# Full attention's value products in pieces of 256 queries, and a choice between streams that counts ScalarE's reserve

## The chip, the cores and the metric

The kernel runs on one core of one Trainium2 chip. The metric is the device time of one execution in microseconds, the median of several runs. TensorE (PE in the profile) multiplies, ScalarE (ACT) takes the exponentials, VectorE (DVE) and GpSimd (POOL) do the rest of the arithmetic, SyncE (SP) issues most of the transfers.

## The reference

Four layers stand one behind the other on a sequence of 2048 rows of 512 numbers. Each takes a layer norm of its input and adds its result to it. Layers one and three (A) are full attention with 32 heads of 16 numbers, where all heads share one key and one value head. Layers two and four (B) have 32 heads with keys and values of their own. They go through the sequence in four segments of 512: causal attention within the segment, mixed by a gate for each head with a linear-attention memory of the segments before.

```python
def _A_ref(x, wq, wk, wv, wo):
    q = (x @ wq).reshape(B, S, H, Dh).transpose(0, 2, 1, 3)
    k = x @ wk
    v = x @ wv
    p = softmax(einsum("bhqd,bkd->bhqk", q, k) * Dh ** -0.5)
    o = einsum("bhqk,bkd->bhqd", p, v)
    return o.transpose(0, 2, 1, 3).reshape(B, S, H * Dh) @ wo

# B, for each of 4 segments s of L = 512
p = softmax(einsum("bhqd,bhkd->bhqk", qs, ks) * scale + mask)
a_dot = einsum("bhqk,bhkd->bhqd", p, vs)
a_mem = (phi(qs) @ M) / (phi(qs) @ z + 1e-6)
outs.append(g * a_mem + (1.0 - g) * a_dot)
M = M + einsum("bhld,bhle->bhde", phi(ks), vs)
z = z + einsum("bhld->bhd", phi(ks))

x = x + _A_ref(layernorm(x), ...)
x = x + _B_ref(layernorm(x), ...)
x = x + _A_ref(layernorm(x), ...)
x = x + _B_ref(layernorm(x), ...)
```

## The kernel before

**Two streams.** The program is written by Python generators that emit instructions, and two streams of them are woven together. The first is full attention, on blocks of 512 queries. It is itself two generators. `a_scores` takes a block, four heads and a tile of 128 keys at a time; for each pair of heads it emits eight matmuls (a score group, `qa,kst` in the profile, written by `by_pairs` at L99 and L102) into a pair of PSUM banks, and one exponential of 128x1024 on ScalarE (L751) into a buffer `pa`. `a_products` then multiplies the exponentials of one key tile with the values: eight fp32 matmuls of 64 keys x 17 columns by 512 queries (`pa,va`, in `a_pv` from L772), which add up over 16 key tiles in two PSUM banks of their own. There are 2048 score groups and 1024 products. The second stream, `side`, does all else for one block of 512 rows: the output projection and layer norm (`out_norm`), layer B's segment (`b_block`: projections, the row maxima `b_rowmax` that VectorE reduces at L988, and `b_attend` with its own scores, masks, exponentials at L1027 and value products `pa,vb`), layer B's output projection, and the next full-attention layer's projections (`a_prep`). A projection is twelve matmuls of 128x128 by 512 (`xh,w`, `xl,w` or `w,xh`, `w,xl`, L454).

**Stages.** Stage 0 weaves block 0 of full attention with the preparation of all blocks. In stages 1 to 7 full attention works on one block while `side` works on the block before. The last `side` runs by itself. Within a stage two pairs of PSUM banks hold scores (`layout("ab")`), and nine buffers hold exponentials. A rule in `a_scores` (`gate`, L721) lets full attention begin only the first unit of the next stage's block before that stage has begun.

**What sets the order.** Every generator yields before a piece of work, with a function that says when the piece could begin by clocks that the Python code keeps for each engine (`clk`). A `Need` carries besides the form of TensorE's array that the piece uses: "rows" (64 rows by 32 columns, for scores and value products of full attention), "cols" (128 rows by 32 columns, for the value products of layer B) or "full". `step` (L410) takes the generator whose piece can begin first, with 260 ns added where the form changes, and a term for the lag of one stream behind the other. `par` (L386) does the like within the second stream. So the order of instructions is fixed when the program is built; on the chip each engine works through its own queue in that order and waits on semaphores. In that order one product is one piece of 8 matmuls, and a projection two pieces of 6 (a yield at `kt == 1`).

Of the kernel before, what the change touches and what calls it, by code (L numbers as in the profile page):

```python
# [89 lines left out]
def net_kernel(ctx, tc, x_in, a_wq, a_wk, a_wv, a_wo, b_wq, b_wk, b_wv, b_wo, b_beta, cst, out):  # L90
# [75 lines left out]
    DRAIN = 130.0  # L166
    PVL = 0.0
    PEND = 0.0
    clk = {"pe": 0.0, "act": 0.0, "dve": 0.0, "pool": 0.0}
# [187 lines left out]
    rings = {}  # L357
# [13 lines left out]
    class Need:  # L371


        def __init__(self, at, form):
            self.at, self.form_ = at, form

# [3 lines left out]
        def form(self):  # L380
            return self.form_() if callable(self.form_) else self.form_

    def form_of(need):
        return need.form() if isinstance(need, Need) else "full"

    def par(*gens):  # L386


        live = []
        for g in gens:  # L390
            if g is not None:
                try:
                    live.append([g, next(g)])
                except StopIteration:
                    pass

        def pick():
            ready = [z for z in live if z[1]() <= clk["pe"]]
            same = [z for z in ready if form_of(z[1]) == tiling[0]]
            return (same or ready or [min(live, key=lambda z: z[1]())])[0]  # L400

        while live:
            yield Need(lambda: min(z[1]() for z in live), lambda: form_of(pick()[1]))
            z = pick()
            try:
                z[1] = next(z[0])
            except StopIteration:
                live = [y for y in live if y is not z]

    def step(zs, cost):  # L410

        now = clk["pe"]
        best = None
        for z in zs:
            if z[1] is None:
                continue
            at = z[1]()
            s = max(now, at) + (2 * DRAIN if form_of(z[1]) != tiling[0] else 0.0) + cost(z)
            if best is None or s < best[0]:
                best = s, at, z  # L420
# [24 lines left out]
    def project(out_, lhs_h, lhs_l, rhs_h, rhs_l, need):  # L445

        yield lambda: max(need(), rings["r"].ready())
        i, ps = rings["r"].take()
# [3 lines left out]
        for kt in range(4):  # L452
# [3 lines left out]
            end = pe(660)  # L456
            if kt == 1:
                yield lambda: 0.0
        def release(t):
# [257 lines left out]
    def a_scores(units):  # L717
# [11 lines left out]
        for ui, (L, f, b, n, k0, k1) in enumerate(units):  # L729
# [8 lines left out]
            for kt in range(k0, k1):  # L738
                pe_, te = [], []
                for u in range(2):  # L740
                    yield Need(lambda: max(need, rings["sc"].ready(), exps.ready(), L["kr"][kt // 4], gate(f, n, k1)), form)
                    ring = rings["sc"]
# [21 lines left out]
    def a_products(n):  # L764

        for _ in range(n):
            yield Need(lambda: max(queue[0][-1], pva_free[0] if queue[0][1] else 0.0) if queue else 1e18, "rows")
            a_pv(*queue.pop(0))

    a_ob = {}  # L770

    def a_pv(L, first, kt, x, unit, last, _):  # L772
        f_, b, n, k0, k1 = unit
        gone[f_] = gone.get(f_, 0) + 1
        t, p = divmod(n, 2)
        for j in (2, 3, 0, 1):
            for h in range(2):
                w_ = slice(64 * h, 64 * h + 64)
                together(j == 2 and h == 0, pva[32 * j:32 * j + 17, h, :], lhsT=L["va"][w_, kt, 0:17],
                         rhs=x[j // 2][0][w_, j % 2, :], start=first, stop=last)  # L780
        e = pe(860, "rows")
        for _, i in x:
# [216 lines left out]
    def b_attend(b, n, r, last):  # L999
# [4 lines left out]
        for kt in range(4):  # L1004
            nq = 512 - kt * P
            es, loc = [], ([(0, 0), (1, 0)] if kt < 2 else [(0, 0), (0, nq)])
            for s_ in range(1 if kt >= 2 else 2):
                yield Need(lambda: max(gr[n], rings["sc"].ready(), exps.ready()), "cols" if exact else "rows")
                ring = rings["sc"]
# [22 lines left out]
        pvb, rel = yield from slot(None, max(tl, v_r[0]), "cols")  # L1032
        for part in parts:
            b_pv(t, p, pvb, *part)
        for i in held:
# [242 lines left out]
```

## Time and profile before

| | us |
|---|---|
| median of 3 runs (3176.38 to 3182.36) | 3179.75 |
| the profiled execution's own time | 3173.99 |
| its span, first to last instruction | 3172.1 |
| TensorE busy, whole span | 2799.0 |
| ScalarE busy, whole span | 2325.2 |
| stage 0 and the preparation (0 to 336.8) | 336.8 |
| stages 1 to 7 (336.8 to 2981.3), each | 362.6 to 397.0 |
| the last block's second stream alone (2981.3 on) | 190.8 |

The granted TensorE clock is 0.975 of full speed on average; in the stages it is 0.97 to 1.00, in the last stretch 0.84. Stage boundaries are taken where each 256th exponential of full attention ends.

How to read it: the trace names an engine, a line, what is written and read, and the count. An fp32 matmul of the program stands in the trace as two, one behind the other, so a value product shows as two passes of eight matmuls. The length of a matmul's row holds the way through the array too, so that the distance from one group's start to the next is its price, not its length. L99 marks the first matmul of a group, L102 the rest.

### The profile page before, as it was taken

What the parts mean: (1) busy time and instruction counts of PE and PEld (TensorE: products, weight loads), DVE (VectorE), ACT (ScalarE), POOL (GpSimd) and SP (SyncE); (2) the same over time, 40 slices, a digit from 0 to 9 for tenths busy, and PEclk for the clock granted to TensorE, in tenths of its full rate; (3) what the DMA queues carried; (4) which work ended last, traced back from release to release, by engine and by line L of the source; (5) the groups of instructions that cost most, each with busy time, mean ns of one, the idle gap of its engine ahead of it and who ended that gap; (6) DMA issues with size and microseconds to landing.
All of it is one profiled execution on the core that took longest, in us unless ns stands there. A gap on an engine that the chain in (4) does not pass through costs nothing.

```text
span 3172.1 us, 116270 instructions
## 1 busy us (share of the span) xinstructions
PE 2799.0 (88%) x51714; PEld 1329.8 (42%) x51714; DVE 1656.8 (52%) x4599; ACT 2325.2 (73%) x2583; POOL 396.0 (12%) x569
## 2 busy tenths in 40 slices
PE   6988898899888998889998898988998889988987
PEld 4533344345333454434443343443443334433544
DVE  7621355545655456556465454565445535555465
ACT  4699787876778767787778768668687876878523
POOL 2100010012100121002110020210110003100011
PEclk9999999999999999999999999999999999999978
DMA  4310121012210132102221132311221104311331
GB/s 124 99 42 22 46 63 43 25 50 78 67 39 18 54 91 58 35 15 73 89 63 46 33 108 66 92 47 34 84 63 31 48 12 160 95 48 33 114 106 34
DMA packets 138560, 194.11 MB, mean 61 GB/s; under 512 B 29664, under 2 KB 97088, under 8 KB 138048
## 3 DMA queue, kind: packets, MB, share of 16 engines
q1 hardware_dynamic: 118912, 121.56, 13.1%
q0 software_dynamic: 19136, 65.02, 7.2%
q8 instruction: 407, 6.67, 0.9%
q14 instruction: 105, 0.86, 0.1%
HBM read 126.46 MB, written 60.03 MB: 59 GB/s over the span
## 4 chain that ended last, share of the span: by engine, by line
PE 38%; ACT 31%; issue 15%; DVE 10%; DMA 3%; POOL 2%; SPq 0%; DVEq 0%; ACTq 0%; POOLq 0%
ACT pa L751 28%; PE bank L99 16%; PE bank L454 13%; PE bank L102 7%; DVE mo L988 4%; ACT pa L1027 3%; DVE m L959 1%; POOL w L186 1%; POOL parts L550 1%; DMA xt<-in_A_x_dram 1%; DMA wst<-in_B_wk_dram 1%; PE bank L514 1%; DMA wst<-in_B_wq_dram 1%; DVE parts L552 0%; DVE qf L532 0%
## 5 line engine op out<-in xcount | busy, mean ns | idle before, releaser
L751 ACT ACTIVATE pa<-bank 128x1024 f32<-128x1024 f32 x2048 | 1945.1, 1113 | 470.0 <-PE bank L102 465.5
L102 PE MATMUL bank<-pa,va 64*17 64x512 f32 x14336 | 1107.4, 601 | 0.2 <-DVE t L790 0.2
L99 PE MATMUL bank<-pa,va 64*17 64x512 f32 x2048 | 1065.5, 601 | 15.8 <-DVE ts L789 9.2
L99 PE MATMUL bank<-qa,kst 49*32 49x512 f16 x2048 | 746.1, 383 | 179.4 <-ACT pa L751 150.3
L102 PE MATMUL bank<-qa,kst 49*32 49x512 f16 x14336 | 827.9, 388 | 0.6 <-DVE xt L835 0.6
L988 DVE CUSTOM_DVE_ANT_0 mo<-bank,maskq 128x256 bf16<-128x256 f32 (+3 forms) x896 | 437.9, 489 | 209.5 <-PE bank L102 145.0
L102 PEld LDWEIGHTS <-kst 49*32 49x32 f16 x14336 | 227.5, 90 | 509.5 <-issue 498.7
L99 PE MATMUL bank<-qkb 48*32 48x128 f16 (+7 forms) x1536 | 346.4, 311 | 104.4 <-DVE m L988 46.0
L1027 ACT ACTIVATE pa<-bank 128x1024 f32<-128x1024 f32 (+2 forms) x384 | 323.7, 887 | 127.5 <-PE bank L102 125.1
L102 PE MATMUL bank<-qkb 48*32 48x384 f16 (+7 forms) x6656 | 369.9, 313 | 0.0
L99 PEld LDWEIGHTS <-kst 49*32 49x32 f16 x2048 | 174.3, 92 | 364.9 <-issue 340.3
L454 PE MATMUL bank<-xh,w 128*128 128x512 f32 x832 | 286.7, 409 | 11.6 <-DVE w L318 4.8
L102 PEld LDWEIGHTS bank<-pa,va 64*17 64x17 f32 x14336 | 259.4, 95 | 24.7 <-DVE t L790 8.8
L186 POOL TENSOR_SCALAR w<-wst 128x512 fp32r<-128x512 f32 x160 | 108.4, 679 | 1189.5 <-PE bank L454 1033.3
L454 PE MATMUL bank<-w,xh 128*128 128x512 f32 x752 | 246.7, 408 | 2.5 <-DVE xh L825 1.1
L102 PEld LDWEIGHTS <-qkb 48*32 48x32 f16 (+1 forms) x6656 | 152.8, 94 | 211.6 <-issue 202.6
L99 PEld LDWEIGHTS bank<-pa,va 64*17 64x17 f32 x2048 | 186.7, 94 | 105.7 <-DVE ts L789 14.5
L789 DVE STREAM_TRANSPOSE ts<-bank 128x512 f32<-128x512 f32 x88 | 62.8, 714 | 279.1 <-PE bank L102 278.9
L99 PEld LDWEIGHTS <-qkb 48*32 48x32 f16 (+1 forms) x1536 | 130.1, 96 | 155.0 <-issue 124.5
L454 PEld LDWEIGHTS bank<-xh,w 128*128 128x128 f32 x832 | 158.7, 191 | 80.0 <-issue 30.9
L1038 DVE STREAM_TRANSPOSE t<-bank 128x512 f32<-128x512 f32 x64 | 45.8, 715 | 273.6 <-PE bank L102 273.6
L102 PE MATMUL bank<-pa,vb 128*17 128x384 f32 (+3 forms) x1920 | 171.4, 442 | 8.5 <-ACT pa L1027 7.6
(164 smaller groups left out, 2987.5 us busy)
## 6 DMA issues: line engine op xcount, KB each, us to landing
sb<-parts SPq DMA_DIRECT2D x128, 128.0 KB
qkb<-sb SPq DMA_DIRECT2D x256, 64.0 KB
x<-xt SPq DMA_DIRECT2D x48, 256.0 KB
xt<-x SPq DMA_DIRECT2D x48, 256.0 KB
qa<-sd SPq DMA_DIRECT2D x176, 66.0 KB
wd<-w POOLq DMA_DIRECT2D x20, 512.0 KB, 3.7
w<-wd POOLq DMA_DIRECT2D x18, 512.0 KB, 6.1
xt<-in_A_x_dram SPq DMA_DIRECT2D x32, 256.0 KB
```

The costliest lines, as they stand in the source:

```text
L99: nc.tensor.matmul(*a, **k)
L102: tc.keep_in_program_order(nc.tensor.matmul(*a, **k))
L186: G.tensor_scalar(o, i, 1.0, 0.0, op0=ALU.mult, op1=ALU.add)
L454: T.matmul(ps, lhsT=l_(kt), rhs=r_(kt), start=n == 0, stop=n == 11)
L514: T.transpose(ps[:, k, :], xn[:, k * P:(k + 1) * P], ident)
L550: G.tensor_scalar(parts[:, 0, :], x, up, 0.0, op0=ALU.mult, op1=ALU.add)
L751: A.activation(x, sc, AF.Exp, scale=scale)
L789: V.transpose(ts.rearrange("p a b -> p (a b)"), pva[:, 0, :])
L959: V.reduce_max(m[:, u0:u0 + per, i, qt], ps[:, 0:per * nk].rearrange("p (h k) -> p h k", k=nk), axis=AX.X)
L988: V.tensor_tensor_reduce(out=mo[:, 0:nk], in0=ps[:, o_:o_ + nk], in1=maskq[:, 512 - nk:512], op0=ALU.add, op1=ALU.max, scale=1.0, scalar=- ...
L1027: A.activation(e[:, :, 0:w], sc[:, :, 0:w], AF.Exp, scale=0.25 if exact else 0.25 / (UPB * UPB))
L1038: V.transpose(t1.rearrange("p a b -> p (a b)"), pvb)
```

## The change

**Products in halves.** `a_products` emits a product in two pieces of 256 queries with a yield between them, except for the first product of a unit, which clears the PSUM region and stays whole. The new `a_part` writes a piece; `a_pv` keeps what comes after.

**A cost and a mark for each piece.** A `Need` now also says how long its piece keeps TensorE (`cost_`; 1320 ns where nothing is said) and whether it feeds ScalarE (`feeds_`: scores of both attentions).

**The choice.** `step` works out when ScalarE would be dry, `dry`: 400 ns (`AHEAD`) before ScalarE's clock, or, where later, the time at which a feeding piece can begin. A piece that doesn't feed ScalarE gets 0.3 (`STARVE`) of the time by which its end would pass `dry` added to its score.

**Other yields.** A projection still yields after the second of its four key tiles (`PIECE = 2`). `b_attend`'s value products yield before key tiles 1 and 2 (`BRK`).

```diff
@@ -165,6 +165,10 @@
     LAG = 0.03
     DRAIN = 130.0
     PVL = 0.0
+    PIECE = 2
+    BRK = (1, 2)
+    STARVE = 0.3
+    AHEAD = 400.0
     PEND = 0.0
     clk = {"pe": 0.0, "act": 0.0, "dve": 0.0, "pool": 0.0}
     evac_on = ["dve"]
@@ -371,14 +375,22 @@
     class Need:
 
 
-        def __init__(self, at, form):
-            self.at, self.form_ = at, form
+        def __init__(self, at, form, cost=400.0, feeds=False):
+            self.at, self.form_, self.cost_, self.feeds_ = at, form, cost, feeds
 
         def __call__(self):
             return self.at()
 
         def form(self):
             return self.form_() if callable(self.form_) else self.form_
+
+    def cost_of(need):
+        c = need.cost_ if isinstance(need, Need) else 1320.0
+        return c() if callable(c) else c
+
+    def feeds(need):
+        c = need.feeds_ if isinstance(need, Need) else False
+        return c() if callable(c) else c
 
     def form_of(need):
         return need.form() if isinstance(need, Need) else "full"
@@ -400,7 +412,8 @@
             return (same or ready or [min(live, key=lambda z: z[1]())])[0]
 
         while live:
-            yield Need(lambda: min(z[1]() for z in live), lambda: form_of(pick()[1]))
+            yield Need(lambda: min(z[1]() for z in live), lambda: form_of(pick()[1]), lambda: cost_of(pick()[1]),
+                       lambda: feeds(pick()[1]))
             z = pick()
             try:
                 z[1] = next(z[0])
@@ -411,11 +424,17 @@
 
         now = clk["pe"]
         best = None
+        dry = 1e18
+        for z in zs:
+            if z[1] is not None and feeds(z[1]):
+                dry = min(dry, max(z[1](), clk["act"] - AHEAD))
         for z in zs:
             if z[1] is None:
                 continue
             at = z[1]()
             s = max(now, at) + (2 * DRAIN if form_of(z[1]) != tiling[0] else 0.0) + cost(z)
+            if not feeds(z[1]):
+                s += STARVE * max(0.0, max(now, at) + cost_of(z[1]) - dry)
             if best is None or s < best[0]:
                 best = s, at, z
         s, at, z = best
@@ -444,7 +463,7 @@
 
     def project(out_, lhs_h, lhs_l, rhs_h, rhs_l, need):
 
-        yield lambda: max(need(), rings["r"].ready())
+        yield Need(lambda: max(need(), rings["r"].ready()), "full", 330.0 * PIECE)
         i, ps = rings["r"].take()
         ring = rings["r"]
         ps = out_(ps)
@@ -454,8 +473,8 @@
                 T.matmul(ps, lhsT=l_(kt), rhs=r_(kt), start=n == 0, stop=n == 11)
                 n += 1
             end = pe(660)
-            if kt == 1:
-                yield lambda: 0.0
+            if kt < 3 and kt % PIECE == PIECE - 1:
+                yield Need(lambda: 0.0, "full", 660.0 * PIECE)
         def release(t):
             ring.free[i] = t
         return ps, end, release
@@ -738,7 +757,7 @@
             for kt in range(k0, k1):
                 pe_, te = [], []
                 for u in range(2):
-                    yield Need(lambda: max(need, rings["sc"].ready(), exps.ready(), L["kr"][kt // 4], gate(f, n, k1)), form)
+                    yield Need(lambda: max(need, rings["sc"].ready(), exps.ready(), L["kr"][kt // 4], gate(f, n, k1)), form, 215.0, True)
                     ring = rings["sc"]
                     k, sc = ring.take()
                     ks = L["kst"][:, kt * P:(kt + 1) * P]
@@ -764,21 +783,29 @@
     def a_products(n):
 
         for _ in range(n):
-            yield Need(lambda: max(queue[0][-1], pva_free[0] if queue[0][1] else 0.0) if queue else 1e18, "rows")
-            a_pv(*queue.pop(0))
+            yield Need(lambda: max(queue[0][-1], pva_free[0] if queue[0][1] else 0.0) if queue else 1e18, "rows", 430.0)
+            u = queue.pop(0)
+            for c in (0,) if u[1] else (0, 256):
+                if c:
+                    yield Need(lambda: 0.0, "rows", 430.0)
+                a_part(*u[:4], u[5], slice(c, c + 512 if u[1] else c + 256))
+            a_pv(*u)
 
     a_ob = {}
+
+    def a_part(L, first, kt, x, last, c):
+        for j in (2, 3, 0, 1):
+            for h in range(2):
+                w_ = slice(64 * h, 64 * h + 64)
+                together(j == 2 and h == 0, pva[32 * j:32 * j + 17, h, c], lhsT=L["va"][w_, kt, 0:17],
+                         rhs=x[j // 2][0][w_, j % 2, c], start=first, stop=last and c.stop == 512)
+        pe(860 if first else 430, "rows")
 
     def a_pv(L, first, kt, x, unit, last, _):
         f_, b, n, k0, k1 = unit
         gone[f_] = gone.get(f_, 0) + 1
         t, p = divmod(n, 2)
-        for j in (2, 3, 0, 1):
-            for h in range(2):
-                w_ = slice(64 * h, 64 * h + 64)
-                together(j == 2 and h == 0, pva[32 * j:32 * j + 17, h, :], lhsT=L["va"][w_, kt, 0:17],
-                         rhs=x[j // 2][0][w_, j % 2, :], start=first, stop=last)
-        e = pe(860, "rows")
+        e = clk["pe"]
         for _, i in x:
             exps.free[i] = e + PEND
         e += PEND
@@ -1005,7 +1032,7 @@
             nq = 512 - kt * P
             es, loc = [], ([(0, 0), (1, 0)] if kt < 2 else [(0, 0), (0, nq)])
             for s_ in range(1 if kt >= 2 else 2):
-                yield Need(lambda: max(gr[n], rings["sc"].ready(), exps.ready()), "cols" if exact else "rows")
+                yield Need(lambda: max(gr[n], rings["sc"].ready(), exps.ready()), "cols" if exact else "rows", 400.0, True)
                 ring = rings["sc"]
                 z, sc = ring.take()
                 for u in range(2):
@@ -1031,6 +1058,8 @@
             parts.append((kt, nq, es, loc))
         pvb, rel = yield from slot(None, max(tl, v_r[0]), "cols")
         for part in parts:
+            if part[0] in BRK:
+                yield Need(lambda: 0.0, "cols", part[1] * 4 / 2.4)
             b_pv(t, p, pvb, *part)
         for i in held:
             exps.free[i] = clk["pe"] + PEND
```

Two places of TensorE's order show what moves. The first is in stage 2, where `out_norm`'s output projection (L454, in the changed kernel L473; operands `w` and `xh` or `xl`) meets full attention's products (`pa`, `va`) and scores (`qa`, `kst`). Rows read: line, operation, what is written and read, shape, count. Before, a whole product, and then the projections of three output tiles with nothing between; the first 8 of 24 such rows, 36 matmuls in all:

```order
L99 MATMUL bank<-pa_11889,va_23_123 17x512
L102 MATMUL bank<-pa_11889,va_23_123 17x512 x3
L102 MATMUL bank<-pa_11879,va_23_123 17x512 x4
L454 MATMUL bank<-w_11652,xh_156 128x512 x2
L454 MATMUL bank<-w_11652,xl_157 128x512
L454 MATMUL bank<-w_11678,xh_156 128x512 x2
L454 MATMUL bank<-w_11678,xl_157 128x512
L454 MATMUL bank<-w_11781,xh_156 128x512 x2
L454 MATMUL bank<-w_11781,xl_157 128x512
L454 MATMUL bank<-w_11786,xh_156 128x512 x2
L454 MATMUL bank<-w_11786,xl_157 128x512
```

Now, the same projection, of which half a tile stands here behind the two halves of a product and ahead of scores:

```order
L99 MATMUL bank<-pa_13977,va_23_123 17x256
L102 MATMUL bank<-pa_13977,va_23_123 17x256 x3
L102 MATMUL bank<-pa_13967,va_23_123 17x256 x4
L99 MATMUL bank<-pa_13977,va_23_123 17x256
L102 MATMUL bank<-pa_13977,va_23_123 17x256 x3
L102 MATMUL bank<-pa_13967,va_23_123 17x256 x4
L473 MATMUL bank<-w_13817,xh_156 128x512 x2
L473 MATMUL bank<-w_13817,xl_157 128x512
L473 MATMUL bank<-w_13822,xh_156 128x512 x2
L473 MATMUL bank<-w_13822,xl_157 128x512
L99 LDWEIGHTS kst_21_121
L99 MATMUL bank<-qa_26_130,kst_21_121 32x512
```

Scores that stood behind 36 projection matmuls now stand behind six, and the next six come after two score groups and a product.

The second place, on TensorE too, is in the same stage, where `b_rowmax` (operand `qkb`) runs beside full attention. Before, a product between two score groups:

```order
L102 MATMUL bank<-qa_25_129,kst_21_121 32x512
L99 MATMUL bank<-pa_12818,va_23_123 17x512
L102 MATMUL bank<-pa_12818,va_23_123 17x512 x3
L102 MATMUL bank<-pa_12782,va_23_123 17x512 x4
L99 LDWEIGHTS kst_21_121
L99 MATMUL bank<-qa_25_129,kst_21_121 32x512
```

Now, half a product between a score group and a row-maximum group; its other half comes after that group:

```order
L102 MATMUL bank<-qa_26_130,kst_21_121 32x512
L99 MATMUL bank<-pa_15679,va_23_123 17x256
L102 MATMUL bank<-pa_15679,va_23_123 17x256 x3
L102 MATMUL bank<-pa_15661,va_23_123 17x256 x4
L99 LDWEIGHTS qkb_28_132
L99 MATMUL bank<-qkb_28_132 32x512
```

Work of the second stream and scores can now stand between the halves of a product.

## The prediction

> **What bounds the kernel now.** The first view is the page: how busy each engine is, how the chain of work that ended last divides, and the costliest group of ScalarE.
>
> ```profile
> span 3172.1 us, 116270 instructions
> PE 2799.0 (88%) x51714; PEld 1329.8 (42%) x51714; DVE 1656.8 (52%) x4599; ACT 2325.2 (73%) x2583; POOL 396.0 (12%) x569
> PE 38%; ACT 31%; issue 15%; DVE 10%; DMA 3%; POOL 2%; SPq 0%; DVEq 0%; ACTq 0%; POOLq 0%
> L751 ACT ACTIVATE pa<-bank 128x1024 f32<-128x1024 f32 x2048 | 1945.1, 1113 | 470.0 <-PE bank L102 465.5
> ```
>
> Neither TensorE nor ScalarE fills the span, and the chain passes back and forth between them. The second view, the waits in total, says who waits for whom:
>
> ```profile
> ACT pa L751 <- PE bank L102: 465.5, 298, 10.8
> PE bank L99 <- ACT pa L751: 168.0, 451, 5.0
> ACT pa L1027 <- PE bank L102: 125.1, 91, 21.6
> ```
>
> The exponentials (L751 in full attention, L1027 in the windowed one) wait 465.5 + 125.1 = 591 us for scores, in few and long waits; TensorE waits 168 us for ScalarE to free a score buffer. The third view is the busy time by stage, cut where every 256th exponential of full attention ends. Columns after the stretch: its length, then busy us of PE, PEld, DVE, ACT, POOL. Three of the seven like stages:
>
> ```profile
> 709.50:1092.80 383.30, 341.47 (x6435) 159.06 (x6433) 206.44 (x599) 289.50 (x322) 49.25 (x67) 1.00 0.18 52
> 1858.60:2255.60 397.00, 345.67 (x6403) 165.38 (x6388) 214.44 (x591) 287.83 (x318) 51.56 (x73) 0.97 0.24 66
> 2618.20:2981.30 363.10, 328.83 (x6352) 149.68 (x6351) 187.29 (x542) 285.97 (x316) 48.49 (x72) 0.99 0.25 75
> ```
>
> ScalarE has the same 286 to 290 us of work in each; the stages differ by how long it stands dry. As its work does not change, a microsecond less of dry ScalarE is a microsecond of span, as long as nothing else takes the chain. The timeline shows one such wait and gives the prices; rows are start, length, engine and line, count, and in brackets the idle time before.
>
> ```profile
> 732.96 0.59 PE L99 MATMUL bank<-pa,va 64*17 64x512 f32 x1
> 733.51 0.74 PE L454 MATMUL bank<-w,xh 128*128 128x512 f32 x2
> ...
> 741.78 0.40 PE L454 MATMUL bank<-w,xl 128*128 128x512 f32 x1
> 742.11 0.39 PE L99 MATMUL bank<-qa,kst 49*32 49x512 f16 x1
> 742.11 0.41 PE L102 MATMUL bank<-qa,kst 49*32 49x512 f16 x7
> 742.14 0.11 PEld L102 LDWEIGHTS <-kst 49*32 49x32 f16 x7
> 742.33 0.38 PE L99 MATMUL bank<-qa,kst 49*32 49x512 f16 x1
> 742.55 0.59 PE L99 MATMUL bank<-pa,va 64*17 64x512 f32 x1
> 742.55 0.61 PE L102 MATMUL bank<-pa,va 64*17 64x512 f32 x7
> 742.55 0.12 PEld L102 LDWEIGHTS bank<-pa,va 64*17 64x17 f32 x7
> 742.59 1.02 ACT L751 ACTIVATE pa<-bank 128x1024 f32<-128x1024 f32 x1 [8.49 <-PE bank L102]
> 742.98 0.59 PE L99 MATMUL bank<-pa,va 64*17 64x512 f32 x1
> ```
>
> Between 733.51 and 742.11 TensorE runs only projections (L454), and ScalarE stands for 8.49 us. Two other views price a projection matmul (the chain: 24 in 5.61 us) and an exponential (the timeline of ScalarE alone: 29 in 26.71 us):
>
> ```profile
> 761.24 5.61 PE bank L454 x24
> 1899.61 26.71 ACT L751 ACTIVATE pa<-bank 128x1024 f32<-128x1024 f32 x29
> ```
>
> So: a score group of eight matmuls 0.22 us (742.11 to 742.33); a value product two passes of 0.43 us (742.55 to 742.98; each fp32 matmul stands in the trace as two), 0.86 in all; a projection matmul 0.235; an exponential 0.92; a change of the array's form 0.10 (product to projection 733.51 - 732.96 - 0.43 = 0.12, projection to scores 742.11 - 741.78 - 0.235 = 0.09).
>
> **The change, part by part.** *The order.* I go down TensorE's order of both kernels, price every row as above (others by their columns), and add up the work between one group that feeds ScalarE (2048 score groups, and the masks that end a windowed score tile) and the next. What exceeds a reserve T, the work that ScalarE has in hand when the stretch begins, is time in which it runs dry:
>
> | T, us | excess before | excess after |
> |---|---|---|
> | 1.15 | 651 | 634 |
> | 1.3 | 582 | 561 |
> | 1.84 (two whole exponentials) | 435 | 381 |
> | 2.5 | 328 | 256 |
>
> The measured 591 us of waiting lie nearest to T = 1.3, so that row prices the change: 21 us less. Two buffers full, T = 1.84, is the bound on the other side: 54 us less. The shape changes more than the sum: stretches over 5 us fall from 36 to 18, stretches over 1.3 us rise from 351 to 416. The 36 projections above become pieces of six with two score groups between. What stays are the blocks of 42 to 48 projections at the ends of some stages, where full attention may not yet go on: no cost term moves them.
>
> From TensorE's side the same can be counted. In stretches of eight or more score groups with nothing but scores and value products, ScalarE sets the pace and TensorE idles 0.92 - 0.22 - 0.43 = 0.27 us for each score group. 480 groups stand so before, 379 after: 101 x 0.27 = 27 us of idle TensorE filled. The two counts agree; I take the middle, **24 us less**. The 114 further changes of form (910 before, 1024 after, 11 us of TensorE at 0.10) are in the stretches already.
>
> *The pieces.* 936 of 1024 products are cut in two (the 88 first ones of a unit stay whole), which makes 2 x 936 = 1872 further passes, each with eight more weight loads. The columns streamed are the same. What a pass costs beyond them is not in the trace for 64x256, so I bound it. From below: score groups stand 0.22 us apart with eight loads inside, and a half pass has the same length and the same eight loads, so nothing: 0. From above: two passes of 256 columns on cold buffers,
>
> ```profile
> 1041.21 0.63 PE L102 MATMUL bank<-pa,vb 128*17 128x256 f32 x8
> ```
>
> take 0.63 us where one pass of 512 takes 0.61: 0.02 us, in all 37 us. The nearest row is the score group, since most half passes follow another product or a score group back to back; I take 0.005 us, half of what the rows resolve, 9 us, of which TensorE's share of the chain (38%) counts: **4 us more**. The loads' cover is the pass before: 0.12 us of loads lie in 0.43 us now and will lie in 0.215. If that cover went, each pass would show its 0.12 us, which no pair of rows does.
>
> [...]
>
> *The rest.* The projections' break stays after two of four key tiles, so nothing is added there. The breaks in the windowed value products (L1033) let scores in at two more places; they are in the order that I counted. Data and buffers are the same; an exponential's buffer comes free after the second half instead of after the whole, and nine of them cover that. No new wait is added: the second half reads what the first half read. SyncE's and GpSimd's queues issue the same instructions, moved along with the streams; what of them shows would be a late load, and DMA has 3% of the chain.
>
> **The sum**: 3173.99 (the profiled execution's own time) - 24 + 4 = 3154. The median of the runs, 3179.75, lies 5.8 us higher, so the forecast is **3160 us**.
>
> **Rivals.** *Reserve nearer to two exponentials.* If ScalarE mostly has both buffers full when a long stretch begins, T = 1.84 holds: -54 + 4, 3130; at T = 2.5 it is -72 + 4, 3112. For it: the longest stretches are what halves in number. Against: 591 us of waiting fit T = 1.3. *No change.* The long waits come back as short ones: 65 more stretches exceed 1.3 us, and each wait pays the way from the scores to the exponential again (742.11 to 742.59, less the 0.22 us of the group: 0.26 us), 17 us, most of the gain; 3154 + 17 + 6 = 3177. For it: TensorE has 329 to 346 us in stages of 363 to 397, so there is not much idle time left to fill. That the change does not do what it says belongs here: with the blocks of 42 to 48 left whole, the choice by ScalarE's reserve decides only part of the waits. *Slower: the pieces cost.* On TensorE, in full attention, every half pass shows the 0.02 us of the cold row: +37, with the lower gain of T = 1.15, -17: 3174 + 20 + 6 = 3200. It decides from 24/1872 = 0.013 us for each further pass on. For it: half the stream time covers the same loads. [...]
>
> **How the numbers follow.** Forecast (3140 to 3173) 0.40; larger gain (about 3112 to 3140) 0.22; no change 0.19; slower 0.19. About 0.2%, 6 us, is what a measurement of this kernel can tell from no change. Faster 0.62, same 0.19, slower 0.19. The range goes from the T = 2.5 end, 3112, to the slower rival, 3200.
>
> **What would show it.** Right: exponentials wait some 570 us for TensorE instead of 591, in more and shorter waits; half passes stand 0.22 us apart; waits of 8 us remain only at stage ends. Wrong: half passes 0.235 us or more apart (the pieces cost); TensorE waiting for ScalarE for more than the 168 us (the gain turned into its waits); or a stage that ends on the windowed stream's DVE and DMA steps with both engines idle, since the new cost holds that stream back.

## The result, and the profile after

The changed kernel takes 3231.07 us (median of 4 runs, 3224.42 to 3244.41), the kernel before 3178.07 us (4 runs): 53 us more, a ratio of 1.0171 with an interval of 1.0146 to 1.0197. The forecast was 3160 us.

The page of the changed kernel (its profiled execution took 3224.42 us) shows neither TensorE nor ScalarE filling the span, as before, with less of ScalarE in the chain and more of TensorE and of transfers:

```profile
span 3222.6 us, 146158 instructions
PE 2848.9 (88%) x66690; PEld 1552.7 (48%) x66690; DVE 1656.2 (51%) x4599; ACT 2335.4 (72%) x2583; POOL 397.9 (12%) x569
PE 43%; ACT 24%; issue 14%; DVE 11%; DMA 5%; POOL 2%; SPq 0%; DVEq 0%; ACTq 0%; POOLq 0%
```

The waits in total (who waits for whom, us, times, longest) show where the time went. In the changed kernel L770 and L1054 are the exponentials, L1015 the row maxima of the windowed attention, L816 the transposes that empty full attention's PSUM:

```profile
ACT pa L770 <- PE bank L102: 504.2, 406, 8.7
PE bank L99 <- ACT pa L770: 123.3, 334, 2.2
ACT pa L1054 <- PE bank L102: 132.3, 82, 21.3
...
PE bank L99 <- DVE m L1015: 56.2, 113, 2.4
PE bank L99 <- DVE ts L816: 24.7, 12, 7.0
PE bank L706 <- DVE m L1015: 21.9, 24, 2.9
PE bank L99 <- DMA qkb<-sb: 20.6, 6, 6.7
```

The same rows of the kernel before:

```profile
PE bank L99 <- DVE m L988: 46.0, 100, 2.4
PE bank L687 <- DVE m L988: 15.4, 31, 1.3
PE bank L99 <- DVE ts L789: 9.2, 8, 1.7
PE bank L99 <- DMA qkb<-sb: 3.2, 5, 1.3
```

TensorE waits 45 us less for ScalarE (168 to 123), as was meant. But these four of its other waits have grown from 74 to 123 us, 50 us more, and single ones reach 7.0 and 6.7 us; all its waits for VectorE and transfers together grow from 128 to 168 us. While TensorE stands, no scores come out of it: the exponentials wait 637 us instead of 591.

So the waits of TensorE changed places, and their sum did not grow. Span less busy time is 373.1 us of idle TensorE before (3172.1 - 2799.0) and 373.7 us after (3222.6 - 2848.9). What grew is its busy time, by 49.9 us, as much as the span. A part of that is a lower granted clock, 0.964 in this execution against 0.975: if busy time went as one over the clock, 2799.0 us would become 2831, which is 32 of the 50 us, as an estimate. The trace's clock records say the same in another way. Within the span TensorE's clock stands at half speed for 158 us before and for 233 us after, and TensorE is busy in 137 and 198 us of them; half passes stand 0.43 us apart there instead of 0.22 (shown below), so the difference is worth some 31 us, again an estimate. The rest of the 50 us holds the further passes (4 us of busy time by run e1 below: 2803.2) and is otherwise not divided.

The stages that the prediction showed, cut in the same way, where every 256th exponential of full attention ends (length, then busy us of PE, PEld, DVE, ACT, POOL):

```profile
700.20:1097.40 397.20, 355.45 (x8351) 193.03 (x8350) 212.78 (x605) 291.71 (x321) 51.78 (x70) 0.97 0.17 50
1859.50:2272.20 412.70, 356.08 (x8166) 191.53 (x8167) 215.67 (x596) 288.94 (x318) 46.23 (x63) 0.93 0.22 61
2647.90:3023.90 376.00, 337.35 (x8276) 180.95 (x8273) 186.93 (x542) 288.72 (x317) 48.47 (x72) 0.96 0.24 73
```

They are 13 to 16 us longer with ScalarE's work nearly unchanged. TensorE's busy time in them is 9 to 14 us longer, and the granted clock (third number from the end) 0.03 to 0.04 lower. A stage that the prediction did not show went the other way, before and after:

```profile
1477.30:1858.60 381.30, 344.28 (x6287) 160.44 (x6294) 211.61 (x587) 287.85 (x317) 51.38 (x70) 0.97 0.22 65
1487.00:1859.50 372.50, 340.24 (x8091) 183.63 (x8083) 207.89 (x581) 287.85 (x318) 52.57 (x70) 1.00 0.23 67
```

Here the clock is 0.03 higher and the stage 8.8 us shorter.

Two places of the changed kernel's timeline show the new waits. In the first, TensorE is to transpose the row maxima (L706) of a unit whose last four maxima VectorE is still taking:

```profile
835.13 1.92 ACT L770 ACTIVATE pa<-bank 128x1024 f32<-128x1024 f32 x2
835.87 0.42 DVE L1015 CUSTOM_DVE_ANT_0 mo<-bank,maskq 128x256 bf16<-128x256 f32 x1
836.21 0.08 DVE L1015 DVE_READ_ACCUMULATOR2_ANT m<- 128x1 f32 x1
836.33 0.42 DVE L1015 CUSTOM_DVE_ANT_0 mo<-bank,maskq 128x256 bf16<-128x256 f32 x1
836.68 0.08 DVE L1015 DVE_READ_ACCUMULATOR2_ANT m<- 128x1 f32 x1
836.90 0.42 DVE L1015 CUSTOM_DVE_ANT_0 mo<-bank,maskq 128x256 bf16<-128x256 f32 x1
...
837.37 0.42 DVE L1015 CUSTOM_DVE_ANT_0 mo<-bank,maskq 128x256 bf16<-128x256 f32 x1
837.72 0.08 DVE L1015 DVE_READ_ACCUMULATOR2_ANT m<- 128x1 f32 x1
837.86 0.28 PE L706 MATMUL bank<-cs,m 128*16 128x128 f32 x1 [2.90 <-DVE m L1015]
...
838.50 0.39 PE L99 MATMUL bank<-qa,kst 49*32 49x512 f16 x1
839.04 1.02 ACT L770 ACTIVATE pa<-bank 128x1024 f32<-128x1024 f32 x1 [2.00 <-PE bank L102]
```

One maximum of 256 keys takes 0.46 us from start to start within a bank (835.87 to 836.33) and 0.57 us where the next one reads another bank (836.33 to 836.90), four 1.9 us. TensorE stands for 2.90 us in front of the transpose, with scores (838.50) queued behind it, and ScalarE runs dry for 2.00 us. The planner's formula for that maximum, 65 + 1.05 x 256, gives 334 ns.

In the second place TensorE waits for the transposes that free full attention's PSUM banks, and VectorE's queue has a weight tile ahead of them, which waits for GpSimd, which waits for a transfer:

```profile
807.07 0.61 POOL L190 TENSOR_SCALAR w<-wst 128x512 fp32r<-128x512 f32 x1 [2.37 <-DMA wst<-in_B_wq_dram]
807.72 0.69 DVE L292 TENSOR_TENSOR w<-wst,w 128x512 fp32r<-128x512 f32 x1 [3.45 <-POOL w L190]
808.67 0.62 POOL L190 TENSOR_SCALAR w<-wst 128x512 fp32r<-128x512 f32 x1 [0.99 <-DMA wst<-in_B_wk_dram]
809.32 0.69 DVE L292 TENSOR_TENSOR w<-wst,w 128x512 fp32r<-128x512 f32 x1 [0.92 <-POOL w L190]
809.93 0.71 DVE L816 STREAM_TRANSPOSE ts<-bank 128x512 f32<-128x512 f32 x1
810.57 0.68 DVE L817 STREAM_TRANSPOSE t<-bank 128x512 f32<-128x512 f32 x1
810.70 1.03 PE L99 MATMUL bank<-pa,va 64*17 64x512 f32 x1 [4.11 <-DVE ts L816]
```

In both places the clock records turn to half speed soon: in the second during the wait (from 808.67 to 815.50), in the first behind it (from 839.39 to 842.80). The last row above shows it, 1.03 us for a matmul that mostly takes 0.59 in the kernel before. After the first place half passes stand 0.43 us apart (840.64 to 841.07), where they stood 0.22 apart just before (838.73 to 838.95).

### The profile page after: what moved, and what is told of

Its sections match the earlier page's. It is cut to its first block, busy times and chain, and to the rows that moved or that the text cites. A ratio compares the mean times of both kernels' runs of the same rounds, so it can differ in the third digit from the quotient of the medians.

```text
span 3222.6 us, 146158 instructions
## 1 busy us (share of the span) xinstructions
PE 2848.9 (88%) x66690; PEld 1552.7 (48%) x66690; DVE 1656.2 (51%) x4599; ACT 2335.4 (72%) x2583; POOL 397.9 (12%) x569
## 4 chain that ended last, share of the span: by engine, by line
PE 43%; ACT 24%; issue 14%; DVE 11%; DMA 5%; POOL 2%; SPq 0%; DVEq 0%; ACTq 0%; POOLq 0%
ACT pa L770 20%; PE bank L99 19%; PE bank L473 13%; PE bank L102 9%; DVE mo L1015 4%; ACT pa L1054 4%; DMA wst<-in_B_wk_dram 1%; DVE m L986 1%; POOL w L190 1%; DMA sb<-parts 1%; PE bank L533 1%; DVE qf L551 1%; DMA wst<-in_B_wo_dram 1%; POOL parts L569 1%; DMA xt<-in_A_x_dram 0%
## 5 line engine op out<-in xcount | busy, mean ns | idle before, releaser
L770 ACT ACTIVATE pa<-bank 128x1024 f32<-128x1024 f32 x2048 | 1949.6, 1108 | 510.3 <-PE bank L102 504.2
L102 PE MATMUL bank<-pa,va 64*17 64x256 f32 (+1 forms) x27440 | 1181.0, 396 | 0.0
L99 PE MATMUL bank<-pa,va 64*17 64x256 f32 (+1 forms) x3920 | 1119.1, 396 | 34.6 <-DVE ts L816 24.7
L99 PE MATMUL bank<-qa,kst 49*32 49x512 f16 x2048 | 743.7, 387 | 135.1 <-ACT pa L770 104.6
L1015 DVE CUSTOM_DVE_ANT_0 mo<-bank,maskq 128x256 bf16<-128x256 f32 (+3 forms) x896 | 439.1, 490 | 266.2 <-PE bank L102 203.6
L102 PEld LDWEIGHTS bank<-pa,va 64*17 64x17 f32 x27440 | 497.1, 95 | 43.4 <-DVE t L817 8.8
L99 PEld LDWEIGHTS bank<-pa,va 64*17 64x17 f32 x3920 | 356.8, 95 | 276.5 <-DVE ts L816 31.7
L99 PE MATMUL bank<-qkb 48*32 48x512 f16 (+7 forms) x1536 | 370.0, 316 | 118.9 <-DVE m L1015 56.2
L1054 ACT ACTIVATE pa<-bank 128x1024 f32<-128x1024 f32 (+2 forms) x384 | 323.5, 890 | 134.2 <-PE bank L102 132.3
L102 PEld LDWEIGHTS <-kst 49*32 49x32 f16 x14336 | 238.0, 91 | 339.9 <-issue 327.2
L102 PE MATMUL bank<-qkb 48*32 48x512 f16 (+7 forms) x6656 | 397.9, 317 | 0.6 <-issue 0.6
L473 PE MATMUL bank<-xh,w 128*128 128x512 f32 x832 | 290.9, 410 | 11.0 <-DVE w L322 4.8
L99 PEld LDWEIGHTS <-kst 49*32 49x32 f16 x2048 | 173.5, 93 | 227.2 <-issue 147.2
L102 PEld LDWEIGHTS <-qkb 50*32 50x32 f16 (+1 forms) x6656 | 157.5, 95 | 228.6 <-issue 221.5
L473 PE MATMUL bank<-w,xh 128*128 128x512 f32 x752 | 251.4, 415 | 2.3 <-DVE xh L852 1.1
L473 PEld LDWEIGHTS bank<-xh,w 128*128 128x128 f32 x832 | 157.9, 190 | 77.6 <-issue 34.3
L816 DVE STREAM_TRANSPOSE ts<-bank 128x512 f32<-128x512 f32 x88 | 62.8, 713 | 252.2 <-PE bank L102 252.2
L99 PEld LDWEIGHTS <-qkb 48*32 48x32 f16 (+1 forms) x1536 | 136.8, 97 | 94.0 <-issue 54.6
L292 DVE TENSOR_TENSOR w<-wst,w 128x512 fp32r<-128x512 f32 x160 | 115.4, 722 | 108.3 <-POOL w L190 107.3
```

Of the source, the lines that this page charges most:

```text
L99: nc.tensor.matmul(*a, **k)
L102: tc.keep_in_program_order(nc.tensor.matmul(*a, **k))
L292: V.tensor_tensor(w[:, 1, :], s, f(w[:, 0, :]), op=ALU.subtract)
L473: T.matmul(ps, lhsT=l_(kt), rhs=r_(kt), start=n == 0, stop=n == 11)
L770: A.activation(x, sc, AF.Exp, scale=scale)
L816: V.transpose(ts.rearrange("p a b -> p (a b)"), pva[:, 0, :])
```

## The experiments

Every run is timed against the kernel before on the same chip. Sixteen runs in four groups: the parts of the change, whether an order's time is luck, the planner's count of VectorE's time, and the queue behind weight transfers. In the table the waits are those of both attentions' exponentials for TensorE; before they are 591 us, in the change 637. They come from one profiled execution of each kernel, whose time can lie off the median: 3213.92 us in e3 (median 3205.33), 3173.84 in e11 (3184.74), 3183.69 in e15 (3191.12), 3242.27 in e16 (3222.39).

| run | ratio to before | interval | exponentials wait, us |
|---|---|---|---|
| the change | 1.0171 | 1.0146 to 1.0197 | 637 |
| e1 halves, order of before | 1.0043 | 1.0027 to 1.0058 | 603 |
| e2 choice alone | 1.0056 | 1.0030 to 1.0082 | 602 |
| e3 halves with a yield | 1.0090 | 1.0071 to 1.0109 | 629 |
| e4 before, lag weight 0.031 | 0.9972 | 0.9958 to 0.9986 | 594 |
| e5 change, lag weight 0.031 | 1.0161 | 1.0135 to 1.0187 | 643 |
| e6 change without breaks | 1.0145 | 1.0123 to 1.0166 | 641 |
| e7 change, maxima +230 ns | 1.0008 | 0.9991 to 1.0026 | 602 |
| e8 before, maxima +230 ns | 1.0010 | 0.9994 to 1.0026 | 584 |
| e9 change, weights on GpSimd | 1.0191 | 1.0155 to 1.0227 | 632 |
| e10 before, weights on GpSimd | 1.0167 | 1.0139 to 1.0195 | 624 |
| e11 choice alone, maxima +230 ns | 1.0047 | 1.0028 to 1.0065 | 594 |
| e12 the same, weights on GpSimd | 1.0125 | 1.0095 to 1.0155 | 618 |
| e13 e7 with lag weight 0.031 | 1.0059 | 1.0037 to 1.0082 | 605 |
| e14 change, maxima +115 ns | 1.0086 | 1.0055 to 1.0117 | 621 |
| e15 e3, maxima +230 ns | 1.0062 | 1.0038 to 1.0086 | 588 |
| e16 change, maxima +460 ns | 1.0143 | 1.0120 to 1.0166 | 639 |

### The parts

**e1: halves in the order of before.**

```diff
+        for c in (slice(0, 512),) if first else (slice(0, 256), slice(256, 512)):
             for j in (2, 3, 0, 1):
                 for h in range(2):
-                    ... pva[32 * j:32 * j + 17, h, :], rhs=x[j // 2][0][w_, j % 2, :]
+                    ... pva[32 * j:32 * j + 17, h, c], rhs=x[j // 2][0][w_, j % 2, c]
```

> The order of before, with each of the 936 products written as two halves one behind the other and nothing let in between. If the further 1872 passes cost what my upper row showed (0.02 us each), and most of it lands on the chain: 15 to 37 us slower than before, V passes 0.235 us apart, and perhaps a lower granted clock than 0.975. If the loss of 53 us lies in the order of the work (TensorE reaching work that hangs on VectorE and on transfers too early): within 10 us of before, half passes 0.215 us apart, the waits of TensorE for VectorE as before.

Measured: 3188.35 us against 3176.96, 11 us slower, between the two bounds. The timeline of this run shows what the passes cost:

```profile
1031.86 0.38 PE L99 MATMUL bank<-pa,va 64*17 64x256 f32 x1
...
1032.08 0.37 PE L99 MATMUL bank<-pa,va 64*17 64x256 f32 x1
1032.08 0.09 PEld L99 LDWEIGHTS bank<-pa,va 64*17 64x17 f32 x1
1032.10 0.39 PE L102 MATMUL bank<-pa,va 64*17 64x256 f32 x7
1032.10 0.11 PEld L102 LDWEIGHTS bank<-pa,va 64*17 64x17 f32 x7
1032.30 0.37 PE L99 MATMUL bank<-pa,va 64*17 64x256 f32 x1
...
1032.51 0.38 PE L99 MATMUL bank<-pa,va 64*17 64x256 f32 x1
...
1032.73 0.38 PE L99 MATMUL bank<-qa,kst 49*32 49x512 f16 x1
```

Four half passes take 0.87 us (1031.86 to 1032.73), two whole ones 0.86. The weight loads are covered: the eight of a pass take 0.13 us (1032.08 to 1032.21) while a pass runs (1032.08 to 1032.30). 11 us over 1872 passes is 6 ns each. A few instructions of the other stream also stand elsewhere in this run, so that even the 11 us are not the passes alone. The halves by themselves cost a fifth of the loss at most.

**e2: the choice alone, e3: halves with a yield.**

```diff
 # e2
-            for c in (0,) if u[1] else (0, 256): ...
+            a_part(*u[:4], u[5], slice(0, 512))
-    BRK = (1, 2)
+    BRK = ()
 # e3
-    STARVE = 0.3
+    STARVE = 0.0
-    BRK = (1, 2)
+    BRK = ()
```

> Only the choice by ScalarE's reserve: products whole, no breaks in the windowed value products. If the new term itself moves TensorE into VectorE's and the transfers' waits: 25 to 55 us slower than before, with the waits of TensorE for the transposes (DVE ts) and row maxima (DVE m) higher than the 9 and 46 us of before and more half-clock windows. If the pieces carry the loss: within 10 us of before, or up to 25 us faster, as the count of the order for the change would have it.

> Only the products in halves with a yield between them, no reserve term (factor 0), no breaks. If the pieces carry the loss, by letting other work between halves: 25 to 55 us slower than before. If the reserve term carries it: within 10 us of before. If any new order costs or gains a per cent by luck: something else than both, with stalls at other places.

Measured: 13 us slower (3190.23) and 28 us slower (3205.33). e2 lies between its bounds; e3 lies at the low end of the one that blames the pieces, and is half of the loss. So the loss is in no single part. Halves, their yield and the choice add up to 11 + 17 + 13 = 41 us.

The two parts lose in different ways, as far as one profile of each can say. In e3 TensorE is idle for 394 us, 21 more than before, at a clock of 0.973. In e2 it is idle for 373.4 us, as before, and busy for 2815.0, 16 us more, at 0.971; the waits that e2 was to raise did rise, for row maxima (L99 and L706 together) from 61 to 82 us and for the transposes from 9 to 17. These are about the waits of the change (78 and 25), with a quarter of its loss.

**e6: the change without the breaks in the windowed products** (`BRK = ()` alone).

> The change without the breaks in the windowed value products. Halves (11 us), their yield (17) and the choice (13) add up to 41 of the change's 53 us. If the breaks carry the other 12: about 40 us slower than before. If the parts make each other worse: still 50 us slower or more.

Measured: 3227.14 us, 49 us slower, not told apart from the change. No effect of the breaks is seen, and the other parts together cost some 8 us more than their sum of 41, which is no more than the intervals allow.

### Luck

An order written by a planner can meet long waits or miss them by chance. Two runs change a number that says nothing new, in both kernels:

```diff
-    LAG = 0.03
+    LAG = 0.031
```

> The kernel before with the planner's weight on the lag of the streams at 0.031 in place of 0.03, which says nothing new and only moves some choices. If the order of before owes its time to luck (long stalls that happen not to meet), this lands 20 to 60 us slower, like the change. If an order's time is set by its rules, it stays within 10 us of before.

> The changed kernel with the planner's weight on the lag at 0.031 in place of 0.03. If the change's order loses by its rules: 35 to 65 us slower than before, like the change, with the same kinds of long waits at other places. If the change met an unlucky order: within 20 us of before.

Measured: before 3165.33 us, 12 us faster (both guesses missed, and nothing speaks for a lucky order of before), the change 3229.28 us, 52 slower, as expected if its rules cost it the time. With one other order for each kernel, luck is worth about 0.3% here, 0.5% with e13 below; the change's loss is three times that.

### VectorE's time in the planner

The planner adds 65 + 1.05n ns to VectorE's clock for a row maximum over n keys, 401 ns for the mean of 320 keys. The groups of the kernel before show what one takes:

```profile
L988 DVE CUSTOM_DVE_ANT_0 mo<-bank,maskq 128x256 bf16<-128x256 f32 (+3 forms) x896 | 437.9, 489 | 209.5 <-PE bank L102 145.0 <-ACT pa L751 1.8 <-DVE m L988 1.3
L988 DVE DVE_READ_ACCUMULATOR2_ANT m<- 128x1 f32 x896 | 73.6, 82 | 0.0
```

I added 489 ns, 82 ns for reading the maximum and a gap of some 60 ns, and took the planner to be 230 ns short. The sum is not right: the reading begins some 74 ns before the other row ends (836.21 against 836.29 above). From the start of the one to the end of the other the trace has 299, 432, 565 and 698 ns for 128, 256, 384 and 512 keys, 98 ns over the formula on average, and then a gap of 34 ns within a bank or 144 ns before the next bank. By the order of the jobs that is some 600 ns for each maximum where they stand back to back, about 200 ns more than the planner has, 896 times. The runs below add 230. So the planner believes the score banks of the row maxima to be free, and the unit to be done, earlier than they are.

```diff
-                e = on("dve", e, 65 + 1.05 * nk)
+                e = on("dve", e, 295 + 1.05 * nk)
```

> The change, but the planner counts each row maximum on VectorE 230 ns longer, as long as the trace shows it (128x256: 423 ns, 82 ns for reading the maximum, and the gap; the planner has 334). If TensorE stands in VectorE's queue because the planner believes row maxima to be ready too early: the waits for DVE m fall from 83 us to under 60, and 10 to 30 us of the 53 come back. If the loss lies elsewhere: within 10 us of the change, 45 to 65 us slower than before.

> The kernel before with the same corrected count of row maxima. If the wrong count costs the old order too: 5 to 25 us faster than before. If only the new choice, which leaves no slack, pays for it: within 10 us of before.

Measured: the change with this one number 3179.86 us, level with before (1.0008, 0.9991 to 1.0026); the kernel before with it 3180.98 us, no different. Of the change's loss, 51 us come back, well over the 10 to 30 expected, and the old order did not need the number. The waits in the corrected change, and TensorE's busy time from its page:

```profile
PE bank L99 <- ACT pa L770: 137.7, 367, 2.3
PE bank L99 <- DVE m L1015: 48.5, 66, 2.5
...
PE bank L99 <- DMA qkb<-sb: 18.9, 7, 8.1
PE bank L99 <- DVE ts L816: 15.9, 8, 6.5
PE bank L706 <- DVE m L1015: 7.2, 13, 0.9
...
span 3179.6 us, 146132 instructions
PE 2823.3 (89%) x66690; PEld 1553.5 (49%) x66690; DVE 1656.1 (52%) x4599; ACT 2332.6 (73%) x2583; POOL 396.3 (12%) x569
```

Those for row maxima fell by 22 us to 56 (61 with a third row, which the 83 of the expectation counts) and from 137 times to 79, those for the transposes by 9 us; the exponentials wait 602 us, 34 less. TensorE is idle for 356.3 us (3179.6 - 2823.3), 17 less than in the change and than before. Its busy time is 24 us above before; at its granted clock of 0.965 the 2799.0 us of before would be 2828, by the same estimate as above. So in this order idle time was filled, and busy time grew by about as much, which by that estimate is the lower clock.

Is it the cause, or one lucky order? Four more runs: another order (e13, lag weight 0.031), half the dose (e14, 180 + 1.05n), twice the dose (e16, 525 + 1.05n), and the dose in e3, where only the halves and their yield are (e15).

> The change with the right count of row maxima (which took 51 us back), and the lag weight at 0.031. If the right count repairs the order by its rule: within 15 us of before again. If that run was a lucky order: 30 us slower than before or more.

> The change with half of the correction, 115 ns in place of 230 for each row maximum. If the too short count causes the loss: between the change and the corrected run, 15 to 40 us slower than before, with the waits for DVE m between 64 and 86 us. If the corrected run was luck: anywhere, most likely near the change (45 us or more).

> The change with each row maximum counted 460 ns longer than the planner has it, twice the correction. If more distance between a row maximum and what needs it keeps helping: 5 to 20 us faster than the corrected run. If the right count is the best one: 5 to 30 us slower than the corrected run, since the windowed stream then falls behind.

> Halves with a yield, no reserve term, no breaks, and the right count of row maxima. Without the right count this was 28 us slower than before. If the wrong count hurts whatever lets TensorE run on between halves: within 12 us of before. If it hurts only together with the reserve term: still 20 to 35 us slower.

Measured: 3189.84 us (18 slower than before), 3201.6 (29), 3222.39 (50) and 3191.12 (19). The change is 53 us slower with no dose, 29 with half, 2 and 18 with 230 ns in two orders, and 50 again with twice of it. The two orders with 230 ns lie 16 us apart, and the two without (53 and 52) lie above both by more than that: the planner's count, and not one order met by chance, takes most of the loss back. Of the four counts the one nearest to the measured length is the best. In e3 the count took 28 us down to 19, with intervals that overlap. e13 missed its bound of 15 us by 3, e15 lies between its two bounds, and e16 is far slower than either of its guesses allowed.

What the count works through is not shown. It moves the whole order, and the waits for row maxima do not follow the loss: e14 has 56 us of them, as e7 has, and is 27 us slower (64 to 86 were expected); e16 has 39 us, the fewest, and is 50 us slower than before; e2 has 82 us with a loss of 13; in the kernel before the count took them from 61 to 42 us (e8) without any gain.

In the choice alone it did nothing:

> The choice by ScalarE's reserve with products whole, no breaks, and row maxima counted as long as they are. If the halves cost 11 to 28 us also here, as alone, and the right count repairs the choice: 10 to 30 us faster than before. If the right count only repairs what the halves spoil: within 10 us of the choice alone, 13 us slower than before.

Measured: 3184.74 us against 3171.54, 13 us slower, as without it (ratios 1.0047 and 1.0056), though the waits for row maxima fell from 82 to 53 us. What the 13 us of the choice by itself are is not shown. The clock is the nearest suspect: e2's five executions have 0.963 to 0.971 and e11's ten 0.964 to 0.973, the kernel before on the same two chips 0.971 to 0.979, and among e11's own executions the fastest (3173.84 us) has the highest clock, 0.973, and the slowest (3198.21) the lowest, 0.964. No run holds the clock and changes the order.

### The queue behind weight transfers

```diff
-        V.tensor_tensor(w[:, 1, :], s, f(w[:, 0, :]), op=ALU.subtract)
-        on("dve", 0.0, 602)
+        G.tensor_tensor(w[:, 1, :], s, f(w[:, 0, :]), op=ALU.subtract)
```

> The change, but the low part of each loaded weight tile is taken on GpSimd instead of VectorE, so that no VectorE instruction stands behind a weight transfer. If the long waits for the transposes of full attention (DVE ts, 25 us, up to 7.0 us each) come from VectorE's queue standing at such an instruction: DVE ts falls below 12 us and 10 to 25 us come back. If not: within 10 us of the change (53 us slower than before).

> The same move in the kernel before, where DVE ts is 9 us and the waits for DVE pk, behind the same instruction, 10 us. If it is worth something there too: 5 to 15 us faster than before. If the old order has slack enough: within 6 us.

> The same with the weights' low part on GpSimd. If both queue effects on VectorE add up: another 5 to 20 us faster than the run without it. If GpSimd's queue then delays the parts of the projections (POOL parts) and with them the transfers to the windowed attention: no gain or a loss, with higher waits for DMA qkb.

Measured: 3230.43 us (59 slower than before on its chip, a ratio of 1.0191; the change has 1.0171, within the intervals), 3224.01 us (52 slower than before, outside both guesses) and 3211.93 us (27 slower than e11). A row of the changed kernel with the move (e9) suggests why it is a bad test:

```profile
L292 POOL TENSOR_TENSOR w<-wst,w 128x512 fp32r<-128x512 f32 x160 | 215.6, 1348 | 10.5
```

On GpSimd the instruction takes 1348 ns, on VectorE some 730 (731 in the kernel before, 722 in the change), so that it can delay what stands behind it there. In the old order the move costs 52 us. In the change the waits for the transposes fell only to 18.9 us, above the 12 that I had set, and in e12 the waits for `qkb` did not grow (9.7 us in e11, 6.7). So the timeline shows that queue, but how much of the loss it makes was not settled.

## Why the prediction was wrong, step by step

*That dry ScalarE is span* held for the change: the exponentials wait 46 us more and the kernel takes 53 us more, and in the runs the two mostly move together (e7 602 us, e14 621, the change 637). They need not: e8 and e15 wait less than before (584 and 588 us) and are no faster.

*That long waits become more and shorter ones* held in form: 406 instead of 298 at L770 (e7: 423), the longest 8.7 us instead of 10.8. Their sum rose instead of falling.

*That TensorE's idle time at full attention's pace is filled* held for that one wait, and by more than the 27 us I counted: it waits 45 us less for ScalarE. But its idle time as a whole stayed where it was, at 373 us.

**The step that failed is the count down TensorE's order**, "24 us less", together with "no new wait is added". I priced each row of the order by TensorE's own rows at full clock, and so took TensorE to be held by nothing but ScalarE, and every idle microsecond that I filled to be won. The runs showed two things in its place. The idle time came back as waits for VectorE and transfers, 40 us more of them against 43 us less for ScalarE in all. And TensorE's busy time, which the sum took to change by the pieces alone, grew by 50 us, some 32 of them by the estimate from the clock.

How the first comes about can be read in the timeline: TensorE stands for 2.90 us, until 837.86, in front of a transpose that needs VectorE, and the scores behind it in the order begin at 838.50. What it had waited for ScalarE was also time in which VectorE took row maxima and transposes and transfers landed. The planner could have kept TensorE from such places, but it has a row maximum some 200 ns too short. That this count matters is shown, 51 us by e7; that it matters through these waits is an argument, and the runs with other counts speak against the waits for row maxima alone. With 230 ns more the change is level with before, at a lower clock and with 17 us less of idle TensorE. No run with the new choice came out faster than before.

*The pieces*: 4 us forecast, 11 measured in e1 (some of it the few moved instructions), within the bounds of 0 and 37. For each further pass e1 shows 6 ns.

*The rivals*: the slower one named the pieces, which by themselves are a fifth of the loss; its 3200 us fell short by 31. The range ended there, because no case priced a wait for another engine or a lower clock, though the last lines named such a wait as a way to be wrong. I asked what covers a price when it is added, and did not ask what the idle time that I filled had covered.

*The clock* stands nowhere in the sum. The trace's clock records stand at half speed for stretches of 3.4 us and mostly multiples of it, 30 of them before and 38 in the change; in the 3.4 us ahead of them TensorE is busy for 43% of the time in the median of the change, against 95% in the median of all such windows. So, as an inference from these medians, a long wait of TensorE may cost twice: while it lasts, and in the slow stretch behind it; no run shows that the wait is the cause. The clock is not what sets the change apart from e7: at the same 0.965 an execution of the change takes 3224.79 us and one of e7 3181.38. But e7's executions, 0.963 to 0.972, also lie mostly below before, 0.971 to 0.977 on that chip, and within each kernel the slower executions are mostly those of the lower clock (the change: 3224.79 us at 0.965, 3244.41 at 0.957). How much of the 53 us is the clock's own, and how much goes with the waits, stays open.

## What to carry to other kernels

An engine's idle time in a fixed order can be another engine's slack, and filling one wait is no gain until the engine's idle time as a whole falls. Before filling it, look in the trace at what the idle engine's next instructions need, how long the engine that delivers it takes for each, and whether the planner has that length. After a change, compare the engine's idle time, its busy time and its granted clock one by one: here the first stayed at 373 us and the second carried the loss. A planner with less slack can need truer times: the same short count cost the old order nothing and the new one 51 us.

## What the runs showed of the hardware that was not expected

Cutting products into passes of 256 columns cost 6 ns a pass in e1 (11 us over 1872 passes), with the 0.13 us of eight weight loads of 64x17 hidden in each 0.215 us. On VectorE the row that reads a maximum begins some 74 ns before the row that computes it ends, so that their lengths may not be added. In the half-speed stretches half passes stand 0.43 us apart instead of 0.22. A subtraction of 128x512 takes 1348 ns on GpSimd and some 730 on VectorE. The old kernel with a lag weight of 0.031 is 0.28% faster than with 0.03 (0.9972, 0.9958 to 0.9986), a gain of the same size as the scatter between orders.
